# Two tiles' values together, output projections one or two steps later, and the head in a new order

## The chip, the cores and the metric

One core of one Trainium2 chip runs the program. It has five engines that work side by side, each with its own instruction queue: TensorE (PE, matmuls; its weight loads are PEld), VectorE (DVE), ScalarE (ACT), GpSimd (POOL) and SyncE (SP, which here only issues DMAs). The metric is the device time of one execution in microseconds.

## The reference

Two stages follow each other. The first is retention: causal attention whose scores are multiplied by a decay per head instead of a softmax. The second is a mixture of four attention experts, of which each token uses the two with the largest gate logits. The work here: 8 batches, 8 heads, 576 tokens, 64 numbers per head, 512 per token.

```
scores = scale * np.matmul(q, k.transpose(0, 1, 3, 2))
Dmat = np.where(rel >= 0, gamma[:, None, None] ** rel[None, :, :], 0.0)
x = np.matmul(scores * Dmat[None], v)          # to [8, 576, 512]

logits = x @ w_gate                            # top 2 of 4, softmax of the two: w, mask
for e in range(E):
    q, k, v = x @ wq[e], x @ wk[e], x @ wv[e]  # 64 wide
    scores = scale * (q @ k.transpose(0, 2, 1))
    a = softmax(causal(scores))
    ye = a @ v @ wo[e]
    out += mask[..., None] * w[:, :, kk:kk + 1] * ye
```

## The kernel before, in words

A batch of 576 tokens is cut into five chunks (128, 128, 128, 128 and 64 tokens), 40 chunks in all. For the projections it is cut into two ranges, the first of 256 tokens (chunks 0 and 1) and the second of 320 (chunks 2 to 4). The main loop (L506) runs over steps n = 0 to 41, and each step does something for several chunks:

- `load(n+2)` issues the DMAs of a later chunk on SP; `decay(n+1)` scales its `vk` by the decay (L106; GpSimd for n above 5, VectorE before), and in the first batch makes a piece of the table `gi` (L105).
- `qk(n)` multiplies queries and keys within blocks of 64 (L139), ScalarE evicts them to `p` (L142), GpSimd makes them causal (L145). `state(n)` (L119) sums up keys and values for later chunks (`st`, added into `s` at L127).
- `result(n-1)` finishes retention for the chunk before: `old` (L167, from `s`) and `own` (L177, from `p` and `vk`), added into x (L170, L182), times `gi` (L187), split into a high part `xh` (L188, ScalarE) and the rest `xl` (L189). It is a generator: the first part runs at the start of a step, the rest in its middle.
- `scores(m)` for the tile m = n - 6: the attention scores of 128 queries (`ss`, L318 or L327), VectorE's maximum (L339), ScalarE's exponential (L347); `normal(m)` scales the rows by the gate's weight over the sum (L369).
- `turn(m-1)`: the tile before is transposed on TensorE (`pt`, L382) and copied to `pth` (L385 on VectorE, L387 on ScalarE).
- `work(n)`: a table (L441) gives steps their projections. For batch b: k and q of the first range at step 5b+3 (`kq0`, L228), its values at 5b+5 (`v0`, L252), k and q of the second range at 5b+6, its values at 5b+7, output projection (`po`, L428, and DMA out) of the first range at 5b+9 and of the second at 5b+12. `vproj` also copies the gate's logits (`lg`, L257).
- `values(m-1)`: probabilities times values (`ys`, L403), evicted by ScalarE (L416) and split by GpSimd (L417, L418).

All four compute engines run their instructions in the order in which the code is written; a program adds only the semaphores for what depends on what. Every PSUM tile is one bank, and all take turns in the same eight banks (`bank`, L48):

```
    def bank(shape, name):
        return pool.tile(shape, F32, name=name, tag="b")
```

So the first matmul into a tile waits until the tile eight allocations earlier has been evicted. The names `x1h`, `x1l` are `xh` and `xl` of the second range. The engines' order in a step after the head is: `qk`, `old`, `own`, `st`, `ss`, `pt`, the step's projections, `ys`. The weights are cast by ScalarE (high part, L213) and subtracted by VectorE or GpSimd (low part, L214).

Of the kernel before, what the change touches and what calls it, by code (L numbers as in the profile page):

```python
# [8 lines left out]
F32 = mybir.dt.float32  # L9
# [19 lines left out]
def f(ap):  # L29
    return ap.bitcast(F32)  # L30
# [3 lines left out]
def kernel(ctx: ExitStack, tc: tile.TileContext, xf, xt, vkf, vkt,  # L34
# [61 lines left out]
    def decay(n):  # L96
        if n >= NC:
            return
        c = n % 5
        t0, C = CH[c]  # L100
        k = C // 64
        vv = VK[n][:, :, 0]
        if 0 < n < 5:
            for kc in range(4):
                act(gi[:, kc, t0:t0 + C], gi[:, kc, :C], AF.Copy, scale=fac[:, c, kc:kc + 1])  # L105
        (gp if n > 5 else v).tensor_mul(vv, vv, gam[:, 2 * c:2 * c + k].unsqueeze(3).to_broadcast([128, k, 4, D]))  # L106

    def state(n):
# [39 lines left out]
    def result(n):  # L148
        b, c = divmod(n, 5)
        t0, C = CH[c]  # L150
        q = 0 if c < 2 else 1
        q0, w, tiles = RNG[q]
        if c == tiles[0]:
            XR[b, q] = X1 if q else [sa.tile([128, 4, w], F32R, name="x" + y, bufs=1) for y in "hl"]
        xh, xl = XR[b, q]
        old = [bank([128, 2, C], "old") for g in range(2)]
        x, p, vk = X[n], P.pop(n), VK[n]
        x32 = sa.tile([128, 2, 2, C], F32, name="x32", tag="x32", bufs=2)
        f0 = 64 if c == 0 else 0
        for s in range(C // 64):  # L160
            k = 2 * c + s
            i = slice(64 * s, 64 * s + 64)
            if k:
                for r in range(2):
                    for g in range(2):
                        for u in range(2):
                            mm(old[g][HALF[u], r, i], S_[b, k - 1][HALF[g], r, u], x[HALF[g], 0, 2 * r + u, i],  # L167
                               start=True, stop=True)
        for g in range(2):
            act(x32[:, g, :, f0:], old[g][:, :, f0:], AF.Copy)  # L170
        own = [bank([128, 2, C], "own") for r in range(2)]
        for s in range(C // 64):
            i = slice(64 * s, 64 * s + 64)
            for g in range(2):
                for r in range(2):
                    for u in range(2):
                        mm(own[r][HALF[u], g, i], vk[HALF[r], s, 0, 2 * g + u], p[HALF[r], g, s, u],  # L177
                           start=True, stop=True)
        for r in range(2):
            if f0:  # L180
                v.tensor_copy(x32[:, :, r, :f0], own[r][:, :, :f0])
            v.tensor_add(x32[:, :, r, f0:], x32[:, :, r, f0:], own[r][:, :, f0:])  # L182
        x32 = x32.rearrange("p g r i -> p (g r) i")
        l0 = t0 - q0
        yield
        e = gp if n > 1 else v
        e.tensor_mul(x32, x32, gi[:, :, t0:t0 + C])  # L187
        act(xh[:, :, l0:l0 + C], x32, AF.Copy)  # L188
        e.tensor_sub(xl[:, :, l0:l0 + C], x32, f(xh[:, :, l0:l0 + C]))  # L189
        yield  # L190

# [10 lines left out]
        RAW[n] = raw = ld.tile([128, kc, w], F32, name="raw", bufs=3)  # L202
        nc.sync.dma_start(raw, wraw[:, o:o + kc * w].rearrange("p (k w) -> p k w", k=kc))

    def weights(n):
        o, kc, w = WCUT[n]
        raw = RAW[n]
        wt = w if n != "v" else NWV
        hi = const.tile([128, kc, wt], F32R, name="wh" + n)
        lo = const.tile([128, kc, wt], F32R, name="wl" + n)  # L210
        W[n] = (hi, lo)
        for r, cs in [(raw, slice(0, w))] + ([(rg, slice(w, wt))] if n == "v" else []):
            act(hi[:, :, cs], r, AF.Copy)  # L213
            (gp if n == "q" else v).tensor_sub(lo[:, :, cs], r, f(hi[:, :, cs]))  # L214

    def proj(b, r, w, p):
        r0, n, tiles = RNG[r]
# [20 lines left out]
    def vproj(b, r, t):  # L238
# [3 lines left out]
        l0, ti = t0 - r0, t - tiles[0]  # L242
        xh, xl = XR[b, r]
        if ti == 0:
            VN[b, r] = (sb.tile([128, nt, E * D], F32, name=f"vn{r}", bufs=2 - r),
                        sb.tile([128, nt, E], F32, name="lg", tag="lg"))
        vn, lg = VN[b, r]
        ps = bank([128, NWV], "pv")
# [122 lines left out]
    def turn(m):  # L371
        b, t = divmod(m, 5)
        p32, sm, n = SS.pop(m)
        nj = t + 1
        pth = sb.tile([128, n, nj, 128], F32, name="pth", tag="pth", bufs=2)
        PT[m] = pth
        for e in range(n):
            for j0 in range(0, nj, 4):
# [59 lines left out]
    for b in range(B):  # L438
        late = b == B - 1

        for n, kind in ((5 * b + 3, "kq0"), (5 * b + 5 - late, "v0"), (5 * b + 6, "kq1"), (5 * b + 7, "v1"),  # L441
                        (5 * b + 9 + (b == B - 2), "o0"), (5 * b + 12, "o1")):
            if b or kind[-1] == "1" or kind == "o0":
                STEPS.setdefault(n, []).append((b, kind, None))

# [51 lines left out]
            run(outproj(b, 1, d))  # L497

    warm(12)
    load(0)  # L500
    load(1)
    nc.sync.dma_start(gi[:, :, :128], gi_d)
# [3 lines left out]
    for n in range(NC + 2):  # L506
# [10 lines left out]
        if n < 3:  # L517

            next(late, None)
            qk(n)  # L520
            state(n)
            run(late)
        else:
            if n < NC:
                qk(n)
            next(late, None)
            if n < NC:
                state(n)
        soft = scores(new[0]) if new else iter(())
        turns = (None for m in old for _ in turn(m))  # L530
        for i, _ in enumerate(soft):
            if i:
                next(turns, None)
        run(late)
        decay(n + 1)
        run(turns)
        gates()
        for w in {1: "kq", 2: "v", 6: "o"}.get(n, ""):
            weights(w)
        for m in new[1:]:  # L540
            run(scores(m))
        for m in new:
            normal(m)
        run(work(n))
        for m in old:
            values(m)
    end()


# [53 lines left out]
```

## Time and profile before

| | us |
|---|---|
| median of 3 runs | 472.93 (472.51 to 473.53) |
| profiled execution | 470.27 |
| its span, first to last instruction | 468.5 |
| PE busy | 450.1 |
| DVE busy | 323.8 |
| ACT busy | 260.0 |
| POOL busy | 219.1 |

The profile is one execution. The span leaves out what lies around the first and the last instruction, so it is a little shorter than the execution's own time. Engine rows add up the time in which an engine had an instruction; a busy engine is not an engine at its best. One batch, five steps, takes some 54 us of the span.

### The profile page before, as it was taken

To read this page: it belongs to the slowest core of one execution; us is meant where nothing else is said; L and a number is where in the kernel's file an instruction comes from. 1 tells how busy PE (TensorE), PEld (TensorE's weight loads), DVE (VectorE), ACT (ScalarE), POOL (GpSimd) and SP (SyncE) were. 2 spreads that over 40 slices of the span, in tenths; PEclk is the share of its full clock that TensorE was granted. 3 is DMA by queue.
4 is the path that set the end of the run, shared out by engine and by line. 5 is a ranking of instruction groups with operands and counts; after the bars stand their busy time and mean duration, and the time that the engine had idled before them with its cause. 6 is when DMAs were issued, how large, how long until landed. Compare 5 with 4: busy or idle time off the path is not lost.

```text
span 468.5 us, 19045 instructions
## 1 busy us (share of the span) xinstructions
PE 450.1 (96%) x7996; PEld 398.9 (85%) x7996; DVE 323.8 (69%) x1136; ACT 260.0 (55%) x814; POOL 219.1 (47%) x285
## 2 busy tenths in 40 slices
PE   7497999999999999999999999999999999989996
PEld 4496988899879998899888998899988998777885
DVE  2644788766797668976687658976679657883662
ACT  2653666555666456645574555754565555663472
POOL 2437464644564454654455445654546544511100
PEclk9689999999999999999999999999999999999999
DMA  8946223314252243414233143512423110010031
GB/s 285 367 162 222 92 93 114 116 48 148 92 203 72 92 123 118 136 48 149 94 135 106 39 147 110 205 50 93 146 93 136 48 59 3 1 47 1 2 102 56
DMA packets 22516, 50.98 MB, mean 109 GB/s; under 512 B 2720, under 2 KB 11680, under 8 KB 22432
## 3 DMA queue, kind: packets, MB, share of 16 engines
q1 hardware_dynamic: 22432, 49.77, 30.7%
q8 instruction: 63, 1.03, 0.9%
q14 instruction: 21, 0.17, 0.1%
HBM read 40.33 MB, written 9.44 MB: 106 GB/s over the span
## 4 chain that ended last, share of the span: by engine, by line
PE 88%; DVE 3%; ACT 3%; POOL 2%; DMA 2%; issue 1%; SPq 0%; ACTq 0%; POOLq 0%; DVEq 0%
PE pj L228 22%; PE po L428 11%; PE pv L252 11%; PE pt L382 10%; PE ys L403 10%; PE ss L318 8%; PE qk L139 4%; PE ss L327 3%; PE own L177 3%; PE st L119 3%; PE old L167 3%; DMA gi<-gi 2%; POOL x L187 1%; DVE p L369 1%; ACT gi L105 1%
## 5 line engine op out<-in xcount | busy, mean ns | idle before, releaser
L347 ACT ACTIVATE p<-p,nm 128x128 f32<-128x128 f32 (+4 forms) x144 | 83.0, 578 | 79.2 <-DVE nm L339 57.7
L369 DVE TENSOR_SCALAR p<-p,sm 128x128 f32<-128x128 f32 (+4 forms) x144 | 78.9, 607 | 1.4
L417 POOL CAST yh<-y 128x256 fp32r<-128x256 f32 (+1 forms) x39 | 16.8, 430 | 109.6 <-ACT y L416 109.6
L339 DVE CUSTOM_DVE_ANT_0 p<-ss,mask 128x512 f32<-128x512 f32 (+3 forms) x128 | 56.4, 483 | 7.8 <-PE ss L318 7.3
L382 PEld LDWEIGHTS pt<-con,p 128*128 128x128 f32 x400 | 43.1, 141 | 20.5 <-issue 12.0
L145 POOL TENSOR_SCALAR_AFFINE_SELECT p<-p 64x512 f32<-64x512 f32 (+1 forms) x80 | 49.5, 619 | 22.7 <-ACT p L142 20.1
L182 DVE TENSOR_TENSOR x<-x,own 128x256 f32<-128x256 f32 (+1 forms) x80 | 26.4, 363 | 48.2 <-ACT x L170 46.7
L189 POOL TENSOR_TENSOR x1l<-x,x1h 128x512 fp32r<-128x512 f32 (+1 forms) x24 | 26.6, 1106 | 62.8 <-ACT x1h L188 62.8
L382 PE MATMUL pt<-con,p 128*128 128x128 f32 x400 | 52.8, 278 | 1.6 <-DVE nm L339 1.2
L403 PE MATMUL ys<-pth,vn 128*64 128x128 f32 (+1 forms) x960 | 53.0, 260 | 0.0
L403 PEld LDWEIGHTS ys<-pth,vn 128*64 128x64 f32 x960 | 44.3, 137 | 5.9 <-issue 1.5
L187 POOL TENSOR_TENSOR x<-x,gi 128x512 f32<-128x512 f32 (+1 forms) x38 | 44.7, 1177 | 4.1 <-DVE x L182 0.5
L318 PE MATMUL ss<-k,q 64*64 64x512 f32 (+3 forms) x512 | 42.5, 432 | 0.0
L385 DVE COPY pth<-pt 128x512 f32<-128x512 f32 (+3 forms) x80 | 37.9, 486 | 4.9 <-PE pt L382 4.4
L106 POOL TENSOR_TENSOR vk<-vk,con 128x512 f32<-128x512 f32 (+1 forms) x34 | 34.0, 1000 | 0.0
L387 ACT ACTIVATE pth<-pt 128x512 f32<-128x512 f32 (+3 forms) x80 | 33.1, 420 | 0.9 <-PE pt L382 0.8
L189 POOL TENSOR_TENSOR xl<-x,xh 128x512 fp32r<-128x512 f32 x14 | 18.8, 1342 | 31.5 <-ACT xh L188 31.5
L142 ACT ACTIVATE p<-qk 128x256 f32<-128x256 f32 (+1 forms) x80 | 24.6, 360 | 11.6 <-PE qk L139 11.6
L416 ACT ACTIVATE y<-ys 128x256 f32<-128x256 f32 (+1 forms) x39 | 14.2, 363 | 28.8 <-PE ys L403 28.8
L428 PE MATMUL po<-yh,who 128*128 128x320 f32 (+1 forms) x128 | 28.8, 306 | 0.6 <-ACT yh L412 0.6
L256 ACT ACTIVATE vn<-pv 128x256 f32<-128x256 f32 x40 | 15.1, 383 | 24.8 <-PE pv L252 24.8
L177 PE MATMUL own<-p,vk 64*64 64x64 f32 x1152 | 26.7, 223 | 2.0 <-issue 1.6
(112 smaller groups left out, 1044.7 us busy)
## 6 DMA issues: line engine op xcount, KB each, us to landing
x<-xf SPq DMA_DIRECT2D x32, 512.0 KB, 4.4
vk<-vkf SPq DMA_DIRECT2D x32, 512.0 KB, 5.4
out<-ot SPq DMA_DIRECT2D x32, 160.0 KB, 1.9
out<-ot SPq DMA_DIRECT2D x32, 128.0 KB, 1.8
raw<-wraw SPq DMA_DIRECT2D x4, 512.0 KB, 7.2
x<-xt SPq DMA_DIRECT2D x8, 256.0 KB, 2.8
vk<-vkt SPq DMA_DIRECT2D x8, 256.0 KB, 3.2
gi<-gi SPq DMA_DIRECT2D x1, 256.0 KB, 7.9
```

Of the source, the lines that this page charges most:

```text
L145: gp.affine_select(w, w, pattern=[[0, 4 * k], [1, 64]], base=0, channel_multiplier=-1, compare_op=OP.is_ge, fill=0.0)
L187: e.tensor_mul(x32, x32, gi[:, :, t0:t0 + C])
L189: e.tensor_sub(xl[:, :, l0:l0 + C], x32, f(xh[:, :, l0:l0 + C]))
L228: mm(ps, ww[:, kc, p * 128:(p + 1) * 128], xx[:, kc, :n], start=(i == 0), stop=(i == 11))
L252: mm(ps, xx[:, kc, l0:l0 + 128], ww[:, kc], start=(i == 0), stop=(i == 11))
L318: mm(ps[2 * p + z][HALF[i]], q[p][HALF[z], l0 + 64 * i:l0 + 64 * i + 64], k[p][HALF[z], :w], start=True, stop=True)
L339: v.tensor_tensor_reduce(p32[:, e], ps[e], mask[:, 512 - w:], -1.0, BIG, OP.add, OP.min, nm[:, e:e + 1])
L347: act(p32[:, e, :w], p32[:, e, :w], AF.Exp, bias=bias, scale=-1.0, accum_out=sm[:, 0, e:e + 1])
L369: v.tensor_scalar(p32[:, e, :t0 + C], p32[:, e, :t0 + C], rs[:, e:e + 1], None, op0=OP.mult)
L382: nc.tensor.transpose(pt[:, j - j0], p32[:, e, 128 * j:128 * j + 128], ident)
L403: mm(py[64 * z:64 * z + 64, p], VN[b, rr][0][:, j - 2 * rr, e * D:(e + 1) * D], src, start=(j == 0), stop=(j == t))
L428: mm(ps, ww[:, p, d * 128:(d + 1) * 128], yy[:, p], start=(i == 0), stop=(i == 5))
```

## The change

It has four parts.

1. `values` no longer runs for one tile at the end of every step. Tiles that have been transposed are collected in a list, and at the end of every odd step (and every step from 40) the values of all tiles in the list are computed one after another. `pth` gets a third buffer, `vn1` a second.
2. The output projections move: the first range's from step 5b+9 to 5b+10, the second range's from 5b+12 to 5b+14.
3. In the first five steps the scaling of `gi` moves from `decay` into `result`, behind the eviction of `old`; the rest of `result` has one more break and, up to step 5, runs at the end of a step.
4. The weights of k and q are split into the casts (`"h"`) and the subtractions (`"l"`), and are made in step 2 instead of 1, those of v in step 3 instead of 2.

```diff
@@ -100,9 +100,6 @@
         t0, C = CH[c]
         k = C // 64
         vv = VK[n][:, :, 0]
-        if 0 < n < 5:
-            for kc in range(4):
-                act(gi[:, kc, t0:t0 + C], gi[:, kc, :C], AF.Copy, scale=fac[:, c, kc:kc + 1])
         (gp if n > 5 else v).tensor_mul(vv, vv, gam[:, 2 * c:2 * c + k].unsqueeze(3).to_broadcast([128, k, 4, D]))
 
     def state(n):
@@ -168,6 +165,9 @@
                                start=True, stop=True)
         for g in range(2):
             act(x32[:, g, :, f0:], old[g][:, :, f0:], AF.Copy)
+        if 0 < n < 5:
+            for kc in range(4):
+                act(gi[:, kc, t0:t0 + C], gi[:, kc, :C], AF.Copy, scale=fac[:, c, kc:kc + 1])
         own = [bank([128, 2, C], "own") for r in range(2)]
         for s in range(C // 64):
             i = slice(64 * s, 64 * s + 64)
@@ -186,6 +186,7 @@
         e = gp if n > 1 else v
         e.tensor_mul(x32, x32, gi[:, :, t0:t0 + C])
         act(xh[:, :, l0:l0 + C], x32, AF.Copy)
+        yield
         e.tensor_sub(xl[:, :, l0:l0 + C], x32, f(xh[:, :, l0:l0 + C]))
         yield
 
@@ -202,16 +203,18 @@
         RAW[n] = raw = ld.tile([128, kc, w], F32, name="raw", bufs=3)
         nc.sync.dma_start(raw, wraw[:, o:o + kc * w].rearrange("p (k w) -> p k w", k=kc))
 
-    def weights(n):
+    def weights(n, parts="hl"):
         o, kc, w = WCUT[n]
         raw = RAW[n]
         wt = w if n != "v" else NWV
-        hi = const.tile([128, kc, wt], F32R, name="wh" + n)
-        lo = const.tile([128, kc, wt], F32R, name="wl" + n)
-        W[n] = (hi, lo)
+        if "h" in parts:
+            W[n] = [const.tile([128, kc, wt], F32R, name="w" + y + n) for y in "hl"]
+        hi, lo = W[n]
         for r, cs in [(raw, slice(0, w))] + ([(rg, slice(w, wt))] if n == "v" else []):
-            act(hi[:, :, cs], r, AF.Copy)
-            (gp if n == "q" else v).tensor_sub(lo[:, :, cs], r, f(hi[:, :, cs]))
+            if "h" in parts:
+                act(hi[:, :, cs], r, AF.Copy)
+            if "l" in parts:
+                (gp if n == "q" else v).tensor_sub(lo[:, :, cs], r, f(hi[:, :, cs]))
 
     def proj(b, r, w, p):
         r0, n, tiles = RNG[r]
@@ -242,7 +245,7 @@
         l0, ti = t0 - r0, t - tiles[0]
         xh, xl = XR[b, r]
         if ti == 0:
-            VN[b, r] = (sb.tile([128, nt, E * D], F32, name=f"vn{r}", bufs=2 - r),
+            VN[b, r] = (sb.tile([128, nt, E * D], F32, name=f"vn{r}"),
                         sb.tile([128, nt, E], F32, name="lg", tag="lg"))
         vn, lg = VN[b, r]
         ps = bank([128, NWV], "pv")
@@ -372,7 +375,7 @@
         b, t = divmod(m, 5)
         p32, sm, n = SS.pop(m)
         nj = t + 1
-        pth = sb.tile([128, n, nj, 128], F32, name="pth", tag="pth", bufs=2)
+        pth = sb.tile([128, n, nj, 128], F32, name="pth", tag="pth", bufs=3)
         PT[m] = pth
         for e in range(n):
             for j0 in range(0, nj, 4):
@@ -439,7 +442,7 @@
         late = b == B - 1
 
         for n, kind in ((5 * b + 3, "kq0"), (5 * b + 5 - late, "v0"), (5 * b + 6, "kq1"), (5 * b + 7, "v1"),
-                        (5 * b + 9 + (b == B - 2), "o0"), (5 * b + 12, "o1")):
+                        (5 * b + 10, "o0"), (5 * b + 14, "o1")):
             if b or kind[-1] == "1" or kind == "o0":
                 STEPS.setdefault(n, []).append((b, kind, None))
 
@@ -497,6 +500,7 @@
             run(outproj(b, 1, d))
 
     warm(12)
+    TURNED = []
     load(0)
     load(1)
     nc.sync.dma_start(gi[:, :, :128], gi_d)
@@ -517,7 +521,10 @@
         if n < 3:
 
             next(late, None)
+            if n == 2:
+                weights("k", "h")
             qk(n)
+            next(late, None)
             state(n)
             run(late)
         else:
@@ -531,19 +538,24 @@
         for i, _ in enumerate(soft):
             if i:
                 next(turns, None)
-        run(late)
+        if n > 5:
+            run(late)
         decay(n + 1)
         run(turns)
         gates()
-        for w in {1: "kq", 2: "v", 6: "o"}.get(n, ""):
-            weights(w)
+        for w in {2: "kq", 3: "v", 6: "o"}.get(n, ""):
+            weights(w, "l" if w == "k" else "hl")
         for m in new[1:]:
             run(scores(m))
         for m in new:
             normal(m)
         run(work(n))
-        for m in old:
-            values(m)
+        run(late)
+        TURNED.extend(old)
+        if n % 2 or n >= NC:
+
+            while TURNED:
+                values(TURNED.pop(0))
     end()
```

What the new order does on ScalarE in the head, steps 0 to 2. Before (`gi` is the decay table, `wh..` a weight's high part, `x<-old` the eviction of `old`):

```order
L105 ACTIVATE gi<-gi,con 128x128 x4
L170 ACTIVATE x_183<-old 128x2x64 x2
L142 ACTIVATE p<-qk 128x256 x2
L188 ACTIVATE xh<-x_183 128x4x128
L105 ACTIVATE gi<-gi,con 128x128 x4
L213 ACTIVATE whk<-raw 128x1024
L213 ACTIVATE whq<-raw 128x1024
L170 ACTIVATE x_285<-old 128x256 x2
L142 ACTIVATE p<-qk 128x256 x2
L188 ACTIVATE xh<-x_285 128x4x128
```

After:

```order
L167 ACTIVATE x_179<-old 128x2x64 x2
L139 ACTIVATE p<-qk 128x256 x2
L188 ACTIVATE xh<-x_179 128x4x128
L167 ACTIVATE x_269<-old 128x256 x2
L170 ACTIVATE gi<-gi,con 128x128 x4
L215 ACTIVATE whk<-raw 128x1024
L139 ACTIVATE p<-qk 128x256 x2
L188 ACTIVATE xh<-x_269 128x4x128
L215 ACTIVATE whq<-raw 128x1024
L236 ACTIVATE k_371<-pj 128x256
```

The eviction `x_285<-old` stood behind a scaling of `gi` and both weight casts; now (as `x_269<-old`) it is ahead of them, and the second cast comes behind the next `xh`.

TensorE at the end of step 12 and the start of step 13, before (the last value projections, then one tile's values, then the next step):

```order
L252 MATMUL pv<-whv,x1l 128x260 x4
L252 MATMUL pv<-whv,x1h 128x260 x4
L252 MATMUL pv<-wlv,x1h 128x260 x4
L252 MATMUL pv<-whv,x1l 128x260 x4
L403 MATMUL ys<-pth,vn_1660 64x128 x4
L139 MATMUL qk<-x 64x64 x16
L167 MATMUL old<-x,s 64x64 x16
L177 MATMUL own<-p,vk 64x64 x16
L119 MATMUL st<-vk 64x64 x16
```

After:

```order
L255 MATMUL pv<-whv,x1l 128x260 x4
L255 MATMUL pv<-whv,x1h 128x260 x4
L255 MATMUL pv<-wlv,x1h 128x260 x4
L255 MATMUL pv<-whv,x1l 128x260 x4
L136 MATMUL qk<-x 64x64 x16
L164 MATMUL old<-x,s 64x64 x16
L177 MATMUL own<-p,vk 64x64 x16
L116 MATMUL st<-vk 64x64 x16
```

The `ys` row has gone from between the value projections and `qk`; the twelve rows of output projection (`po`) that stood ahead of the value projections in this step are gone as well.

TensorE at the end of step 14 and the start of step 15, before (end of the first range's output projection, values, next step):

```order
L428 MATMUL po<-yl_2184,who 128x256 x2
L428 MATMUL po<-yh_2183,wlo 128x256 x2
L403 MATMUL ys<-pth,vn_1660 64x128 x4
L403 MATMUL ys<-pth,vn_2130 64x128 x2
L403 MATMUL ys<-pth,vn_1660 64x128 x4
L403 MATMUL ys<-pth,vn_2130 64x128 x2
L139 MATMUL qk<-x 64x64 x16
L167 MATMUL old<-x,s 64x64 x8
L177 MATMUL own<-p,vk 64x64 x8
L119 MATMUL st<-vk 64x64 x16
```

After:

```order
L431 MATMUL po<-yh_1481,wlo 128x320 x2
L431 MATMUL po<-yh_1481,who 128x320 x2
L431 MATMUL po<-yl_1482,who 128x320 x2
L431 MATMUL po<-yh_1481,wlo 128x320 x2
L136 MATMUL qk<-x 64x64 x16
L164 MATMUL old<-x,s 64x64 x8
L177 MATMUL own<-p,vk 64x64 x8
L116 MATMUL st<-vk 64x64 x16
```

The projection is now that of the second range (320 columns for 256), and `qk` follows it with no `ys` between.

## Rows read from the trace of the kernel before

**Rows 1.** The page: engine table (busy us, share of the span, instructions) and the shares of the chain of waits by engine.

```profile
PE 450.1 (96%) x7996; PEld 398.9 (85%) x7996; DVE 323.8 (69%) x1136; ACT 260.0 (55%) x814; POOL 219.1 (47%) x285
...
PE 88%; DVE 3%; ACT 3%; POOL 2%; DMA 2%; issue 1%; SPq 0%; ACTq 0%; POOLq 0%; DVEq 0%
```

**Rows 2.** Busy time by stretch. Columns: the stretch in us, its length; busy us and instructions (in brackets) of PE, PEld, DVE, ACT and POOL in this order, the granted clock, the DMA share and GB/s. The first two rows are stretches of the head; the last is the sum over five stretches that together are one batch (254.84 to 309.10 us).

```profile
16.33:26.57 10.24, 6.08 (x104) 5.77 (x96) 7.72 (x14) 7.03 (x17) 4.10 (x3) 0.50 0.87 310
26.58:45.00 18.42, 15.23 (x491) 14.05 (x489) 6.69 (x24) 7.96 (x28) 12.29 (x15) 1.00 0.59 202
...
sum 54.26, PE 54.26 PEld 48.87 DVE 39.91 ACT 31.25 POOL 28.33; mean PE 10.85 PEld 9.77 DVE 7.98 ACT 6.25 POOL 5.67
```

**Rows 3.** Timeline of TensorE: groups of value matmuls (`ys`) and the instructions that follow them. Columns here and in all groups below: start us, length us, engine, line, operation, written<-read, shape, count, and in brackets the idle time before and what ended it.

```profile
223.94 0.66 PE L403 MATMUL ys<-pth,vn 128*64 128x128 f32 x8
224.52 0.69 PE L139 MATMUL qk<-x 64*64 64x64 f32 x32
...
234.66 1.09 PE L403 MATMUL ys<-pth,vn 128*64 128x128 f32 x16
235.69 0.46 PE L139 MATMUL qk<-x 64*64 64x64 f32 x16
...
243.07 1.53 PE L403 MATMUL ys<-pth,vn 128*64 128x128 f32 x24
244.53 0.69 PE L139 MATMUL qk<-x 64*64 64x64 f32 x32
...
429.73 1.82 PE L403 MATMUL ys<-pth,vn 128*64 128x64 f32 x48
431.49 1.95 PE L318 MATMUL ss<-k,q 64*64 64x512 f32 x16
```

**Rows 4.** Timeline of TensorE and GpSimd in step 9 and at the start of step 10 (`po` is the first range's output projection of batch 0).

```profile
73.83 1.93 PE L318 MATMUL ss<-k,q 64*64 64x512 f32 x15
76.98 0.48 PE L428 MATMUL po<-yh,who 128*128 128x256 f32 x2
80.00 1.53 PE L403 MATMUL ys<-pth,vn 128*64 128x128 f32 x24
81.25 1.23 POOL L106 TENSOR_TENSOR vk<-vk,con 128x512 f32<-128x512 f32 x1
82.53 0.69 PE L119 MATMUL st<-vk 64*64 64x64 f32 x32
```

**Rows 5.** Step 24 and the start of step 25, TensorE and GpSimd; below them two rows of step 22 (a second-range output projection, the value projection after it).

```profile
236.91 1.93 PE L318 MATMUL ss<-k,q 64*64 64x512 f32 x15
244.33 1.22 POOL L106 TENSOR_TENSOR vk<-vk,con 128x512 f32<-128x512 f32 x1
245.61 0.69 PE L119 MATMUL st<-vk 64*64 64x64 f32 x32
...
215.93 0.53 PE L428 MATMUL po<-yh,who 128*128 128x320 f32 x2
219.53 0.64 PE L252 MATMUL pv<-whv,x1h 128*128 128x260 f32 x4
```

**Rows 6.** Step 22 and the start of step 23 (TensorE and VectorE), and below them the `own` matmuls of step 8.

```profile
214.33 1.08 PE L318 MATMUL ss<-k,q 64*64 64x256 f32 x15
222.13 0.15 DVE L257 COPY lg<-pv 128x4 f32<-128x4 f32 x1
225.51 0.65 PE L177 MATMUL own<-p,vk 64*64 64x64 f32 x31
...
62.38 0.75 PE L177 MATMUL own<-p,vk 64*64 64x64 f32 x30 [0.38 <-DVE lg L257]
```

**Rows 7.** The scaling of p by row (VectorE L369): for a tile of 128 keys in step 6, for one of 256 in step 7, and GpSimd's subtraction beside the latter.

```profile
52.42 0.87 DVE L369 TENSOR_SCALAR p<-p,sm 128x128 f32<-128x128 f32 x4
...
59.06 3.10 DVE L369 TENSOR_SCALAR p<-p,sm 128x256 f32<-128x256 f32 x4
59.17 1.39 POOL L189 TENSOR_TENSOR xl<-x,xh 128x512 fp32r<-128x512 f32 x1 [2.71 <-ACT xh L188]
```

**Rows 8.** Head: steps 1 and 2 on VectorE, ScalarE and TensorE.

```profile
16.80 0.69 DVE L106 TENSOR_TENSOR vk<-vk,con 128x512 f32<-128x512 f32 x1
15.89 1.26 ACT L105 ACTIVATE gi<-gi,con 128x128 f32<-128x128 f32 x4
18.95 0.63 ACT L170 ACTIVATE x<-old 128x256 f32<-128x256 f32 x2
19.61 0.75 DVE L182 TENSOR_TENSOR x<-x,own 128x256 f32<-128x256 f32 x2 [0.26 <-ACT x L170]
21.08 1.04 DVE L187 TENSOR_TENSOR x<-x,gi 128x512 f32<-128x512 f32 x1
22.21 0.63 ACT L188 ACTIVATE xh<-x 128x512 fp32r<-128x512 f32 x1 [2.08 <-DVE x L187]
22.89 1.23 PE L228 MATMUL pj<-xh,whk 128*128 128x256 f32 x4 [4.16 <-ACT xh L188]
24.96 1.05 PE L228 MATMUL pj<-xh,wlk 128*128 128x256 f32 x4
27.67 0.69 PE L139 MATMUL qk<-x 64*64 64x64 f32 x32
```

**Rows 9.** TensorE in steps 4 and 5: two waits.

```profile
38.66 0.68 PE L119 MATMUL st<-vk 64*64 64x64 f32 x28 [1.56 <-DVE lg L257]
...
43.94 0.69 PE L119 MATMUL st<-vk 64*64 64x64 f32 x32 [1.63 <-POOL vk L106]
```

## The prediction

> **What bounds the kernel now.** I read the engine table and the chain of waits first [rows 1]. TensorE is busy 450.1 of 468.5 us, and the chain that ends last is TensorE for 88%: no other engine is a bound on average. Next the busy times by stretch [rows 2]. One batch (five steps) takes 54.26 us, in which TensorE works all the time and VectorE, the next, 39.91 us. Only the head is loose: from 16.33 to 26.57 us TensorE works 6.08 of 10.24 us at a granted clock of 0.50 (its level of 1.2 GHz), and from 26.58 to 45.00 it works 15.23 of 18.42 us. So the change can win TensorE instructions in the steady part and waits in the head. It can lose wherever a step becomes so short on TensorE that another engine is no longer hidden. I therefore looked, step by step, at how late the other engines' results arrive, and expect two such places.
>
> **Values together (A).** A group of value matmuls is followed at once by the next group, so starts can be subtracted [rows 3]: 8 matmuls take 224.52 - 223.94 = 0.58 us, 16 take 235.69 - 234.66 = 1.03, 24 take 244.53 - 243.07 = 1.46. That is 0.44 per 8 and a fixed 0.14 to 0.15 per group. In the tail a group of 48 narrow ones takes 431.49 - 429.73 = 1.76, so length adds no second fixed part. Over steps 7 to 39 there are 33 groups now and 17 after. One of the 16 lost groups belongs to term B, and 15 x 0.15 = 2.2 us saved. The buffers cost nothing: transposed p lives one step longer and has a third buffer, the second range's values have a second one.
>
> **The first batch's output projection (B).** It moves from step 9 to 10, and nothing else is issued in step 9. Now [rows 4] scores start at 73.83, the projection at 76.98 and the values at 80.00, so it takes 3.02 us; `st` of step 10 starts at 82.53. GpSimd's decay of the `vk` that it reads ends at 81.25 + 1.23 = 82.48, which is 8.65 after the scores began. That end doesn't depend on the projection: decay stands on GpSimd behind `xl`, which waits for the ScalarE cast `xh`, which is queued behind the exponentials of this step's scores. So the stretch from scores to `st` stays 8.70 us long though 3.0 us of work leave it, and that work is added to step 10. One tile's values (16 matmuls, 1.03) leave step 8 and fall into the hole in step 9. Net +1.9 us.
>
> **Steps 14, 24, 34 (C).** They lose the first-range projection and one tile's values and get the second-range projection. In step 24 [rows 5] scores start at 236.91, decay ends at 244.33 + 1.22 = 245.55 (again 8.64 later) and `st` starts at 245.61, so even now there is no slack. After the change TensorE needs from scores to `st`: 3.15 up to the projection (76.98 - 73.83), 219.53 - 215.93 = 3.60 for a second-range projection, and 245.61 - 244.53 = 1.08 for `qk`, `old` and `own`; 7.83 in all. It waits 8.70 - 7.83 = 0.87 each time: 3 x 0.87 = +2.6 us. Bounds: nothing, if decay comes earlier by that much; 3 x 1.5, if the chain in front of it slips by one more ScalarE operation of 0.63 (as long as the cast `xh` in [rows 8]).
>
> **Steps 12, 22, 32 (D).** Here the second-range projection leaves and the values go to the odd step, so only three value projections remain. The output of step 22 [rows 6] is the case. Scores start at 214.33; 1.60 later comes what is now the projection and then will be the value projections, which take 223.94 - 219.53 = 4.41; `own` follows 225.51 - 224.52 = 0.99 after `qk`. `own` could start at 221.33. But all PSUM tiles take turns in eight banks, and without a `ys` tile in between `own` falls on the bank of the first value projection. That bank is free when VectorE has copied the gate logits (`lg`), at 222.13 + 0.15 = 222.28, behind the scaling of the whole tile by row. Behind `own` on TensorE stand `st` and the scores. A precedent is in the trace: `own` at 62.38, after a step that has no output projection, waits 0.38 for just that copy. So I price it between 0.38 and 1.0 and take 0.9, nearer to the worked case: 3 x 0.9 = +2.7 us.
>
> **A rule against the last step of that argument.** While GpSimd's subtraction runs (59.17 for 1.39 us), four scalings of 128x256 take 3.10 us; four of 128x128 with no GpSimd beside them take 0.87 [rows 7]. Twice the length costs 3.6 times as much. The Trainium skill, "SBUF — State Buffer", Who interferes with whom, says that a VectorE operation in a two-port mode and a GpSimd operation lock one shared port pair, and the later one blocks fully until the other is done; the rows agree with it. By that rule `lg` would be about 3.10 - 2 x 0.87 = 1.4 us earlier once the subtraction no longer meets the scaling, and D would vanish. I don't expect the meeting to be undone, as both hang on the same exponentials; it is rival two.
>
> **The head (G).** Now [rows 8] ScalarE brings gi(1) (from 15.89), two weight casts and only then `x<-old` at 18.95, so `x<-x,own` starts on VectorE at 19.61, the product with gi at 21.08, `xh` at 22.21 and the projection at 22.89. After the change `x<-old` is ahead of these; VectorE's first free moment is the end of `vk` at 17.49. With the same durations: 17.49 + 0.7 + 1.04 + 0.63 = 19.9, so the projection starts 2.9 earlier. It doesn't keep all of it: its third group needs `wlk`, which VectorE now makes after `s`, `xl` and `vk`, at about 22.9 instead of before 24.96. The last 16 matmuls took 27.67 - 24.96 = 2.71 and 24.96 - 22.89 = 2.07 per 8 at the lower clock, so they end at 25.6 to 27.0; I take 26.2, a gain of 1.5. Up to step 6, waits of 1.56 (`lg`) and 1.63 (`vk`) on TensorE [rows 9] lie open, but the ScalarE to GpSimd chain of `x`, `xh` and the causal select is nearly as long, and I give that stretch 0.5. G = -2.0 us (-1.3 to -3.3).
>
> **Sum.** -2.2 + 1.9 + 2.6 + 2.7 - 2.0 = +3.0 us. The profiled execution took 470.27 us (span 468.5), so its copy would take 473.3. The median of the runs is 472.93, 2.66 more, and the forecast is for a median: 475.9 us. Of the rest I cost at nothing: the odd steps get longer on TensorE, so nothing else can be late there; SP issues the same loads two steps ahead, behind outputs that now come later; the tail is the same code.
>
> **Rivals.**
> 1. Faster: the waits B to D don't open, because the chains of decay and `lg` start earlier than the scores seem to say. Then -2.2 - 2.0 = -4.2 leaves about 468.7, with B's projection moved at no cost. For it: GpSimd is busy 28.33 and VectorE 39.91 of 54.26 us [rows 2], so each has idle time to move into. Against it: `st` starts 0.05 to 0.06 behind decay's end in [rows 4, 5] alike, so it is held already. Chance 0.14.
> 2. No change: D vanishes (the scaling no longer meets the subtraction), 475.9 - 2.7 = 473.2. For it: the size of the slow-down in [rows 7]. Against it: both engines wait for the same ScalarE cast order. Chance 0.13.
> 3. Slower by more: the head gives only 0.7 and the holes grow to 1.5 each in C and D, because ScalarE now gets the evictions of two values tiles at once and the exponentials behind them slip. -2.2 - 0.7 + 1.9 + 4.5 + 4.5 = +8.0, 480.9. It decides from the point at which the first exponential of an even step waits for a `y` eviction and not for VectorE's maximum. Chance 0.05.
> 4. The change doesn't pair at all. The written order fixes 17 groups, so no chance.
>
> **The numbers.** The forecast has 0.68, with its own range 473.5 to 478.5. I widen below to 472.0 for rival two and leave out the rest: 472.0 to 478.8. A measurement tells about 0.2% (0.95 us) from no change, so faster gets 0.14 (rival one), the same 0.14 (rival two and the weakest of the forecast), slower 0.72.
>
> **What would show it.** Right: 17 groups of `ys`; `own` of steps 13, 23 and 33 idle about 0.9 us behind `lg`; `st` of steps 10, 15, 25 and 35 idle behind `vk`; the first projection near 20 us and `qk` after it at 25.6 to 27. Wrong: no idle time ahead of these, a pair of batches not some 1 us longer than 108.5, or a head that gives back 4 us.

## The result and the profile after

The changed kernel took 476.07 us (median of 6 runs, 475.23 to 478.38), the kernel before 473.05 in the same comparison (471.71 to 473.53): ratio 1.0084, 95% interval 1.0064 to 1.0105. It is slower by 3.0 to 5.0 us. Profiled execution against profiled execution it is 475.23 against 470.27, +4.96.

The page after, to be held against [rows 1]:

```profile
PE 447.6 (95%) x7996; PEld 399.0 (84%) x7996; DVE 327.6 (69%) x1136; ACT 260.4 (55%) x814; POOL 220.2 (46%) x285
...
PE 73%; DVE 10%; ACT 9%; POOL 3%; DMA 2%; issue 2%; SPq 0%; DVEq 0%; POOLq 0%; ACTq 0%
```

TensorE is busy 2.5 us less, as values in pairs should make it, yet its share of the chain that ends last fell from 88% to 73%; VectorE and ScalarE have most of the rest. TensorE now waits for the other engines. From the start of step 7 to that of step 39 (columns as in [rows 2]), before:

```profile
52.23:398.43 346.20, 345.82 (x6398) 311.51 (x6397) 255.90 (x904) 199.59 (x634) 180.55 (x228) 1.00 0.31 105
```

and after:

```profile
52.04:399.48 347.44, 340.51 (x6357) 307.86 (x6357) 257.26 (x904) 197.69 (x629) 181.79 (x228) 1.00 0.31 103
```

TensorE idled 0.38 us there and now idles 6.93. Where it waits, its timeline says (columns as in [rows 3]; steps 9 and 10, then the starts of 13, 15, 23 and 33):

```profile
78.31 0.88 PE L406 MATMUL ys<-pth,vn 128*64 128x128 f32 x12 [0.54 <-ACT pth L390]
81.39 0.69 PE L116 MATMUL st<-vk 64*64 64x64 f32 x32 [1.11 <-POOL vk L103]
...
115.24 0.62 PE L177 MATMUL own<-p,vk 64*64 64x64 f32 x26 [0.47 <-DVE lg L260]
...
135.78 0.69 PE L116 MATMUL st<-vk 64*64 64x64 f32 x32 [0.69 <-POOL vk L103]
...
225.19 0.62 PE L177 MATMUL own<-p,vk 64*64 64x64 f32 x26 [1.21 <-DVE lg L260]
...
335.09 0.62 PE L177 MATMUL own<-p,vk 64*64 64x64 f32 x26 [1.21 <-DVE lg L260]
```

With 0.65 and 0.68 for `st` of steps 25 and 35, not shown, these waits add up to 6.56 us. The waits for `vk` and for `lg` are the two kinds that the forecast named, at its places; the 0.54 for a copy of transposed p in step 9 it did not name. The rows that answer to [rows 6, 7], VectorE and GpSimd in step 22:

```profile
221.54 3.44 DVE L372 TENSOR_SCALAR p<-p,sm 128x256 f32<-128x256 f32 x4
224.90 0.28 DVE L260 COPY lg<-pv 128x4 f32<-128x4 f32 x3
...
221.65 1.39 POOL L190 TENSOR_TENSOR xl<-x,xh 128x512 fp32r<-128x512 f32 x1 [2.71 <-ACT xh L188]
222.99 1.09 POOL L103 TENSOR_TENSOR vk<-vk,con 128x512 f32<-128x512 f32 x1
224.17 1.37 POOL L142 TENSOR_SCALAR_AFFINE_SELECT p<-p 64x512 f32<-64x512 f32 x2
```

The same step in the kernel before:

```profile
219.25 2.96 DVE L369 TENSOR_SCALAR p<-p,sm 128x256 f32<-128x256 f32 x4
...
219.36 1.39 POOL L189 TENSOR_TENSOR xl<-x,xh 128x512 fp32r<-128x512 f32 x1 [2.71 <-ACT xh L188]
220.71 1.09 POOL L106 TENSOR_TENSOR vk<-vk,con 128x512 f32<-128x512 f32 x1
```

In both the scaling lies beside two GpSimd operations, the subtraction and the decay. Now it also runs into a third, the causal select of the next step, and is 0.48 us longer. The head, answering to [rows 8]:

```profile
20.97 3.37 DVE L217 TENSOR_TENSOR wlk<-raw,whk 128x1024 fp32r<-128x1024 f32 x1
...
20.44 2.81 POOL L217 TENSOR_TENSOR wlq<-raw,whq 128x1024 fp32r<-128x1024 f32 x1 [0.53 <-POOL p L142]
...
19.40 1.22 PE L231 MATMUL pj<-xh,whk 128*128 128x256 f32 x4 [1.11 <-ACT xh L188]
...
24.39 1.22 PE L231 MATMUL pj<-xh,wlk 128*128 128x256 f32 x4 [2.67 <-DVE wlk L217]
...
28.02 0.69 PE L136 MATMUL qk<-x 64*64 64x64 f32 x32
```

The first projection does start 3.5 us earlier, and then waits 2.67 us for `wlk`, so that `qk` of step 3 comes at 28.02 instead of 27.67. Step 7 begins at 52.04 (52.23 before): of the head's gain 0.2 us is left in this pair of traces. All of the loss is behind it: from step 7 to the end 421.46 us instead of 416.27.

### The profile page after: what moved, and what is told of

Its sections match the earlier page's. It is cut to its first block, busy times and chain, and to the rows that moved or that the text cites. A ratio compares the mean times of both kernels' runs of the same rounds, so it can differ in the third digit from the quotient of the medians.

```text
span 473.5 us, 19049 instructions
## 1 busy us (share of the span) xinstructions
PE 447.6 (95%) x7996; PEld 399.0 (84%) x7996; DVE 327.6 (69%) x1136; ACT 260.4 (55%) x814; POOL 220.2 (46%) x285
## 4 chain that ended last, share of the span: by engine, by line
PE 73%; DVE 10%; ACT 9%; POOL 3%; DMA 2%; issue 2%; SPq 0%; DVEq 0%; POOLq 0%; ACTq 0%
PE pj L231 21%; PE ys L406 9%; PE po L431 9%; PE pt L385 8%; PE pv L255 8%; PE ss L321 5%; ACT p L350 5%; PE ss L330 3%; DVE p L372 3%; PE qk L136 3%; PE own L177 3%; PE st L116 2%; DMA vk<-vkf 2%; DVE x L182 2%; PE old L164 2%
## 5 line engine op out<-in xcount | busy, mean ns | idle before, releaser
L372 DVE TENSOR_SCALAR p<-p,sm 128x128 f32<-128x128 f32 (+4 forms) x144 | 84.3, 645 | 1.4
L142 POOL TENSOR_SCALAR_AFFINE_SELECT p<-p 64x512 f32<-64x512 f32 (+1 forms) x80 | 50.5, 632 | 54.1 <-ACT p L139 51.0
L420 POOL CAST yh<-y 128x256 fp32r<-128x256 f32 (+1 forms) x39 | 15.8, 404 | 76.2 <-ACT y L419 76.1
L406 PE MATMUL ys<-pth,vn 128*64 128x128 f32 (+1 forms) x960 | 49.7, 258 | 0.6 <-ACT pth L390 0.5
L103 POOL TENSOR_TENSOR vk<-vk,con 128x512 f32<-128x512 f32 (+1 forms) x34 | 35.0, 1029 | 0.1
L390 ACT ACTIVATE pth<-pt 128x512 f32<-128x512 f32 (+3 forms) x80 | 33.1, 420 | 0.9 <-PE pt L385 0.8
L116 PE MATMUL st<-vk 64*64 64x64 f32 x1024 | 22.9, 224 | 6.4 <-POOL vk L103 3.6
```

The lines of the kernel that those rows point to most:

```text
L142: gp.affine_select(w, w, pattern=[[0, 4 * k], [1, 64]], base=0, channel_multiplier=-1, compare_op=OP.is_ge, fill=0.0)
L372: v.tensor_scalar(p32[:, e, :t0 + C], p32[:, e, :t0 + C], rs[:, e:e + 1], None, op0=OP.mult)
L406: mm(py[64 * z:64 * z + 64, p], VN[b, rr][0][:, j - 2 * rr, e * D:(e + 1) * D], src, start=(j == 0), stop=(j == t))
```

## The experiments

Each was timed beside the kernel before; ratios are to that. The kernel before had medians of 471.7, 472.9 and 471.7 us in the three sets, so ratios are compared, not times; the changed kernel's, 1.0084, comes from the comparison above.

**wlq on VectorE.**

```diff
-                (gp if n == "q" else v).tensor_sub(lo[:, :, cs], r, f(hi[:, :, cs]))
+                v.tensor_sub(lo[:, :, cs], r, f(hi[:, :, cs]))
```

> The changed kernel, with the low part of q's weights (wlq) subtracted on VectorE behind wlk, not on GpSimd beside it. Theory: in the head of the changed kernel wlk takes 3.37 us (1.22 before) only because GpSimd's wlq runs from 20.44 to 23.25 and holds VectorE up. Then wlk takes 1.2 to 1.3 here, the third group of projections starts near 22.2 instead of 24.39, the qk behind it at 25.6 to 26.3 instead of 28.02, and the kernel is 1.7 to 2.3 us faster than the changed one (473.8 to 474.4). Rival: wlk is slow by itself (its size, or the ScalarE cast whq beside it): it still takes over 3 us, wlq comes after it, the last group starts later still, and the kernel is 0 to 1 us slower than the changed one.

Measured: 474.36 us, ratio 1.0060 (1.0037 to 1.0082), 0.24% or 1.1 us better than the changed kernel. VectorE and TensorE in its head:

```profile
21.16 1.21 DVE L217 TENSOR_TENSOR wlk<-raw,whk 128x1024 fp32r<-128x1024 f32 x1
...
22.42 1.23 PE L231 MATMUL pj<-xh,wlk 128*128 128x256 f32 x4 [0.40 <-DVE wlk L217]
...
26.14 0.96 PE L136 MATMUL qk<-x 64*64 64x64 f32 x32
```

`wlk` takes 1.21 us, and the projection and `qk` come within 0.25 us of what was expected. Step 7 begins at 50.47, 1.6 earlier. The medians show less than that and less than the 1.7 to 2.3 expected, and their intervals overlap. More traces bear the gain out: from the start of step 2 to that of step 7 the four with `wlq` on VectorE, this one and three below, take 33.1 to 34.6 us, the five with the new head and `wlq` on GpSimd 35.0 to 36.2. So the cause is shown, the size, some 1.4, only roughly.

**Decay early.**

```diff
         if n > 5:
+            next(late, None)
+            decay(n + 1)
             run(late)
-        decay(n + 1)
+        else:
+            decay(n + 1)
```

> The changed kernel, with GpSimd's decay of vk (steps from 6) between the product with gi and the subtraction xl, where GpSimd waits 3 us for ScalarE's cast. Theory: st of steps 10, 15, 25 and 35 waits only for this decay; its idle times of 1.11, 0.69, 0.65 and 0.68 go and the kernel is 2.5 to 3.5 us faster than the changed one (472.6 to 473.6); in step 9 up to 0.6 stays, because the values still wait for a copy of transposed p. Rival: the decay now runs beside VectorE's maxima or scalings and slows them, so that lg and own come later: gain under 1 us, with own of steps 13, 23, 33 idle more than now (0.47, 1.21, 1.21).

Measured: 469.85 us, ratio 0.9948 (0.9932 to 0.9964): 1.36% or 6.4 us better than the changed kernel, twice what was expected. Steps 7 to 39 take 340.22 us instead of 347.44. Not only the waits for `vk` went. GpSimd, VectorE and TensorE in step 22:

```profile
216.85 1.05 POOL L103 TENSOR_TENSOR vk<-vk,con 128x512 f32<-128x512 f32 x1
219.61 1.38 POOL L190 TENSOR_TENSOR xl<-x,xh 128x512 fp32r<-128x512 f32 x1 [1.72 <-ACT xh L188]
...
219.50 2.17 DVE L372 TENSOR_SCALAR p<-p,sm 128x256 f32<-128x256 f32 x4
221.59 0.28 DVE L260 COPY lg<-pv 128x4 f32<-128x4 f32 x3
...
221.66 0.85 PE L177 MATMUL own<-p,vk 64*64 64x64 f32 x30
```

With the decay out of its way the same scaling takes 2.17 us and ends before the next select begins, `lg` is in time and `own` waits for nothing. Summed over the kernel, the page's group of the scaling, first of the changed kernel:

```profile
L372 DVE TENSOR_SCALAR p<-p,sm 128x128 f32<-128x128 f32 (+4 forms) x144 | 84.3, 645 | 1.4
```

and with the early decay:

```profile
L372 DVE TENSOR_SCALAR p<-p,sm 128x128 f32<-128x128 f32 (+4 forms) x144 | 66.0, 518 | 1.4
```

The rival (the decay slows the maxima instead) falls.

**Value projections ahead of the scaling.**

```diff
+        job = work(n)
+        if n > 5 and n % 5 == 2 and n % 2 == 0:
+            run(job)
         for m in new:
             normal(m)
-        run(work(n))
+        run(job)
```

> The changed kernel, where in steps 12, 22 and 32 the value projections with their copies of the gate logits (lg) are written ahead of the scaling of p by row, on VectorE thus ahead of it. TensorE's own order is the same. Theory: own of steps 13, 23, 33 waits for lg alone, which stands behind the scaling; its idle times (0.47, 1.21, 1.21) go, and the kernel is 2.5 to 3.6 us faster than the changed one (472.5 to 473.6). Rival: the scaling, now about 1.5 us later, becomes what the transposes of the next step wait for, and the wait moves from own to pt: gain under 1 us.

Measured: 477.36 us, ratio 1.0111 (1.0086 to 1.0136): no gain, if anything a loss. The rival holds. VectorE and TensorE in step 23:

```profile
225.14 1.60 DVE L372 TENSOR_SCALAR p<-p,sm 128x256 f32<-128x256 f32 x4
226.67 0.74 DVE L182 TENSOR_TENSOR x<-x,own 128x256 f32<-128x256 f32 x2
...
227.13 0.77 PE L385 MATMUL pt<-con,p 128*128 128x128 f32 x4 [0.70 <-DVE x L182]
```

`own` is free (223.97), but VectorE still scales when `own` and the scores are done, and the transposes wait. The wait has moved one phase on.

**All three.** The three edits above in one kernel.

> The three edits of the runs beside it in one kernel. If each takes away its own wait and they do not meet, the gains add up: 6.7 to 9.4 us less than the changed kernel, 467 to 469, below the kernel before (473). Rival: with less idle time in TensorE other results come late in turn, and the sum is at most 4 us, about level with the kernel before.

Measured: 470.86 us, ratio 0.9975 (0.9956 to 0.9993), worse than the early decay alone. Between the starts of steps 12 and 14 it takes 21.7 us where the early decay alone takes 20.2: the early decay has already taken away the wait of `own` that the edit before this one was to win back, so only its cost is left. Beside the next run, which lacks that edit, it is 1.0% slower. The gains did not add up: it is 5.2 us faster than the changed kernel, between the theory's 6.7 to 9.4 and the rival's 4.

**wlq and early decay, without the third edit.**

> The changed kernel with two edits: wlq on VectorE behind wlk, and GpSimd's decay of vk ahead of the subtraction xl. Theory: the head gains what it gained alone (1.1 by the medians, about 1.9 by the trace) and the decay what it gained alone (about 6), so the kernel stands 3 to 4.5 us under the kernel before (ratio 0.990 to 0.994). Rival: in the head the gain is eaten up by the later steps 3 to 6, as they wait for GpSimd anyway, and it is no faster than the run with the decay alone (ratio 0.9948).

Measured: 466.59 us, ratio 0.9873 (0.9851 to 0.9895), 6.0 us below the kernel before and the best of all, below the 0.990 to 0.994 expected. The gain is larger than the two alone (0.24% and 1.36% on 1.0084 make 0.9923), by no more than the intervals of the runs add up to. Its chain is TensorE's again:

```profile
PE 88%; DMA 3%; DVE 3%; ACT 3%; POOL 1%; SPq 1%; issue 0%; POOLq 0%; DVEq 0%; ACTq 0%
```

**The early decay in three steps only** (12, 22, 32, where `st` doesn't wait for it).

```diff
-        if n > 5:
-            run(late)
-        decay(n + 1)
+        if n > 5 and n % 10 == 2:
+            next(late, None)
+            decay(n + 1)
+            run(late)
+        else:
+            if n > 5:
+                run(late)
+            decay(n + 1)
```

> The changed kernel with the early decay in steps 12, 22 and 32 alone; there st does not wait for it. Theory of the port: the scaling of p by row is slow (3.44 us for four of 128x256) because it meets two GpSimd operations, the subtraction and the decay; with one of them gone it takes 2.1 to 2.3, lg is about 1.3 earlier, the idle times of own in steps 13, 23, 33 (0.47, 1.21, 1.21) fall to 0.2 or less, and the kernel is 2.5 to 3.5 us faster than the changed one. Waits of st at steps 10, 15, 25, 35 stay as they are. Rival: the scaling is slow by its size; it takes 3 us or more, own waits as before, and the gain is under 0.7.

Measured: 473.26 us, ratio 1.0020 (1.0003 to 1.0036), 0.64% or 3.0 us better than the changed kernel. VectorE and TensorE, first the untouched wait of step 10, then step 22:

```profile
81.11 0.69 PE L116 MATMUL st<-vk 64*64 64x64 f32 x32 [1.11 <-POOL vk L103]
...
223.22 0.85 PE L177 MATMUL own<-p,vk 64*64 64x64 f32 x30
...
221.06 2.17 DVE L372 TENSOR_SCALAR p<-p,sm 128x256 f32<-128x256 f32 x4
```

This is the cleanest of the tests: in these steps no instruction waits for the decay's own result, and taking it out of the scaling's way alone ends the idle time of `own` in all three (0.47, 1.21 and 1.21 in the changed kernel).

**The early decay in the kernel before.** The same edit there, with the break between `xh` and `xl`.

> The kernel before, with only GpSimd's decay of vk (steps from 6) ahead of the subtraction xl. Theory: the early decay is worth something only where a step is too short on TensorE; the kernel before has one recorded wait of that kind after the head (own at 62.38 behind lg, 0.38 us), so it gains 0.3 to 1.0 us (ratio 0.998 to 0.9995). Rival: the decay is a hidden bound of the kernel before too, as its st follows decay by 0.05 us in every short step; then it gains 2 to 4 us (ratio 0.992 to 0.996) and the change is slower even beside the best of its fixes.

Measured: 470.39 us, ratio 0.9954 (0.9938 to 0.9970), in the rival's range. The trace shows less: steps 7 to 39 take 345.66 us (346.20 before), and step 8 alone is 0.67 shorter, although the scaling falls from 78.9 to 65.6 us in this kernel too. Where the rest of the 2.2 us lies, one trace of each doesn't tell; it stays open. So part of what the early decay gives has nothing to do with the change: beside a kernel before that has it too (0.9954), the changed kernel with it (0.9948) is level, and only the run with `wlq` moved as well (0.9873) is ahead.

**The fixed kernel without pairs** (values at the end of every step).

> The fixed kernel (wlq on VectorE, early decay) with the values of one tile at the end of every step, as in the kernel before; head and moved projections stay. Theory: pairing is worth the start of 16 groups, 16 x 0.15, so this is 2.0 to 2.6 us slower than the fixed kernel with pairs. Rival: pairs cost as much elsewhere (the values of two tiles wait for the copy of transposed p in step 9, 0.54 us, and the even steps are short), and it is 0 to 1 us slower.

Measured: 470.09 us, ratio 0.9944 (0.9922 to 0.9965), 0.71% or 3.3 us slower than with pairs. The 2.4 expected for the pairs and 0.8 in step 9 make up the difference: there the values of tile 2 now wait twice for the copies of transposed p, 1.35 us in sum instead of 0.55:

```profile
74.20 0.88 PE L406 MATMUL ys<-pth,vn 128*64 128x128 f32 x12 [0.44 <-ACT pth L390]
75.98 0.88 PE L406 MATMUL ys<-pth,vn 128*64 128x128 f32 x12 [0.91 <-ACT pth L390]
```

**The moves alone**, in the kernel before.

```diff
-                        (5 * b + 9 + (b == B - 2), "o0"), (5 * b + 12, "o1")):
+                        (5 * b + 10, "o0"), (5 * b + 14, "o1")):
```

> The kernel before, with only the output projections moved (first range to step 5b+10, second to 5b+14); values after each step and the old head. Theory: the moves open the holes, the pairs save starts and deepen some holes. Step 9 without a projection: scores to st still 8.70 us, the hole 3.0. Steps 12, 17, 22, 27, 32, 37 have value projections and one tile's values only, like step 7 before: own waits 0.4 to 0.6 behind lg each, 2.4 to 3.6. Steps 14 to 39 with a projection of 320 columns and values are long enough: nothing. So 5.4 to 6.6 us slower than the kernel before (ratio 1.011 to 1.014). Rival: the pairs are what opens the holes; the moves alone cost at most the 3.0 of step 9 (ratio under 1.0065).

Measured: 477.68 us, ratio 1.0124 (1.0104 to 1.0144), as the theory had it. `own` waits for `lg` in the six steps behind those that it named, 0.19 to 0.39 us each. TensorE in steps 9, 10 and 23:

```profile
77.24 0.88 PE L403 MATMUL ys<-pth,vn 128*64 128x128 f32 x12 [0.43 <-ACT pth L387]
79.02 0.88 PE L403 MATMUL ys<-pth,vn 128*64 128x128 f32 x12 [0.91 <-ACT pth L387]
82.09 0.69 PE L119 MATMUL st<-vk 64*64 64x64 f32 x32 [1.09 <-POOL vk L106]
...
226.33 0.81 PE L177 MATMUL own<-p,vk 64*64 64x64 f32 x32 [0.39 <-DVE lg L257]
```

**The pairs with the least moves**, in the kernel before, with the buffers of part 1.

```diff
+                        (5 * b + (9 if b % 2 else 10), "o0"), (5 * b + (13 if b % 2 else 12), "o1")):
...
+        TURNED.extend(old)
+        if n % 2 or n >= NC:
+            while TURNED:
+                values(TURNED.pop(0))
```

> The kernel before, with only the pairs, and output projections moved no further than the pairs need: first range 5b+10 for even b (5b+9 else), second range 5b+13 for odd b (5b+12 else). Theory: 16 starts saved, -2.4; step 9 as in the changed kernel, +1.9; steps 14, 24, 34 have a projection of 256 columns and no values, 3.15 + 3.02 + 1.08 = 7.25 of 8.70 us, so st waits 1.45 each, +4.4; steps 12, 22, 32 keep a projection, nothing. Together +3.9 (ratio 1.007 to 1.010), with st of steps 15, 25, 35 idle by 1.2 to 1.5 behind vk. Rival: without the far moves the pairs gain: -0.5 to -2.4 (ratio under 0.999).

Measured: 480.28 us, ratio 1.0177 (1.0155 to 1.0199), the slowest of all and 4.4 us beyond the theory's +3.9. The waits of 1.3 to 1.4 are there (step 15), but I had overlooked that steps 19 and 29 lose their projection as step 9 does. That makes two more holes of some 1.9 us, like the first one. TensorE in steps 15, 19 and 20:

```profile
140.00 0.69 PE L119 MATMUL st<-vk 64*64 64x64 f32 x32 [1.36 <-POOL vk L106]
...
191.26 0.88 PE L403 MATMUL ys<-pth,vn 128*64 128x128 f32 x12 [0.54 <-ACT pth L387]
194.34 0.69 PE L119 MATMUL st<-vk 64*64 64x64 f32 x32 [1.11 <-POOL vk L106]
```

The far moves of the change are thus the milder form: they keep some work in these steps.

**The head alone**, in the kernel before (parts 3 and 4 of the change).

> The kernel before, with only the new head (order of gi and of the weights); values after each step, projections at their old steps. Theory: the earlier start of the first projection is given back because wlk waits for GpSimd's wlq; qk of step 3 comes at 27 to 28.5 us as in the changed kernel, and the time is -0.5 to +0.5 against the kernel before (ratio 0.999 to 1.001), with wlk at 3.2 to 3.5 us. Rival (my forecast): the head alone gains 1.3 to 3.3 us (ratio 0.993 to 0.997), and the loss came later.

Measured: 471.06 us, ratio 0.9993 (0.9978 to 1.0007). My forecast for the head falls (the interval leaves room for 1.0 us of gain, not for 1.3); the giving back is shown by the same pair of rows, VectorE and GpSimd:

```profile
21.14 3.37 DVE L217 TENSOR_TENSOR wlk<-raw,whk 128x1024 fp32r<-128x1024 f32 x1
...
20.61 2.81 POOL L217 TENSOR_TENSOR wlq<-raw,whq 128x1024 fp32r<-128x1024 f32 x1 [0.54 <-POOL p L142]
```

**The kernel before once more.**

> The kernel before once more, for a second profile, since its profiled execution (470.27) is one of its shortest and its runs reach from 470.2 to 474.0. Theory: the spread is made in the head, by how long TensorE stays at the lower clock: from step 7 on both traces agree within 0.3 us, and a longer execution has its whole difference ahead of 52 us. Rival: in longer executions waits open in the steps as well (own behind lg, st behind vk); then the stretch from step 7 to step 39 (346.2 us in the first trace) is longer by most of the difference.

Measured: ratio 1.0005 (0.9988 to 1.0023), profiled execution 472.27, 2.0 longer than the first one. Steps 7 to 39 agree within 0.1 us (346.30), the head is 0.4 longer, and 1.6 lie where neither theory had them, behind step 39. Two stretches there, columns as in [rows 2], first of the first trace:

```profile
420.00:425.00 5.00, 3.45 (x23) 2.92 (x22) 4.03 (x19) 3.49 (x13) 0.43 (x1) 1.00 0.13 44
425.00:430.00 5.00, 5.00 (x41) 4.81 (x41) 0.28 (x2) 1.04 (x4) 0.00 (x0) 1.00 0.01 3
```

and of the second:

```profile
420.00:425.00 5.00, 3.45 (x20) 2.92 (x19) 3.87 (x19) 3.04 (x12) 0.81 (x2) 0.87 0.20 68
425.00:430.00 5.00, 5.00 (x29) 5.00 (x28) 0.75 (x3) 0.88 (x2) 0.00 (x0) 0.79 0.01 3
```

## Why the prediction was right, and where it was not

The range and the sign held, and 475.9 stands beside 476.07. Of the signs named, a pair of batches (steps 22 to 32) takes 109.90 us instead of 108.53. The steps were not all that good.

**A, values together: right.** The trace has the 17 expected groups. The run without pairs is 3.3 us slower, as 2.4 for 16 starts and 0.8 in step 9 would make it; the starts were not timed apart from the rest.

**B, the empty step 9: right.** Steps 8 to 10 take 30.92 us (30.93 before) although one tile's values, 1.90, have left for step 11: +1.9. The hole is divided between the values, which wait 0.54 for a copy of transposed p, and `st`.

**C, `st` behind the decay: right.** In step 14 `st` starts 8.71 after the scores (127.07 to 135.78; 8.70 forecast). From the start of `own` to `st` it takes 1.1 us where it took 0.33 before (245.28 to 245.61), some 0.8 more in each of three steps, 2.4 in all (forecast 2.6).

**D, `own` behind `lg`: right in kind, too small.** `own` takes 0.7, 1.4 and 1.4 us more (2.7 forecast, 3.5 measured). The step that failed is the one that took the end of `lg` over from the trace before, 7.95 us after the scores. It came 8.4 after them (216.62 to 225.05), because the scaling took 3.44 instead of 2.96. In the trace before it already lay beside the subtraction and the decay. What is new is the causal select: the step is now so short that the select of the next one starts at 224.17, while the scaling runs. In step 12, where the scaling takes 2.97 as before, `own` waits only 0.47.

The prediction also read the 3.10 us of [rows 7] as the cost of the subtraction alone; in that trace the decay (60.52 to 61.61) lay beside it too. So rival two had the mechanism (the scaling meeting GpSimd sets D), but more of GpSimd takes part in it, and the change doesn't undo the meeting. The early decay undoes most of it. Beside the subtraction alone the scaling takes 2.17, beside subtraction and decay 2.96, with the select behind them 3.44, and 1.60 in the run with the projections first, where only the end of the select lies beside it.

Rival three's larger holes came in part, in D, but not by its way: the first exponential of step 22 waits for VectorE's maximum (2.01 us), not for a `y` eviction.

**G, the head: wrong.** -2.0 was forecast, -0.2 came in this pair of traces. Five traces with the old head take 35.6 to 36.2 us from step 2 to step 7 and five with the new one 35.0 to 36.2, so the gain is some 0.4 in the mean and within the spread. The start of the first projection (19.9 forecast, 19.40 measured) and the 0.5 of steps 3 to 6 (24.56 us before, 24.02 after) were right. What failed is the sentence that `wlk` is made "at about 22.9": it is priced there by its length of 1.2 in the trace before. It ends at 24.34, because GpSimd's `wlq`, which before started 1.06 behind it, now starts 0.53 ahead of it. The run with `wlq` on VectorE shows it; the head alone shows the same rows again.

I weighed the Trainium skill, "SBUF — State Buffer", Who interferes with whom, for the scaling alone. The same section says that a VectorE operation with two inputs in SBUF contends with a GpSimd operation that reads SBUF. That is `wlk` beside `wlq`, and the trace agrees: `wlk` ends 1.09 us after `wlq` (24.34 and 23.25), and again 1.09 after it in the head alone (24.51 and 23.42). By this rule the head's gain was to be had only if the two were kept apart, as in the run with `wlq` on VectorE.

**The sum.** With A as forecast and the other terms as measured, -2.2 + 1.9 + 2.4 + 3.5 - 0.2 is +5.4; the scores of step 40 take 2.06 instead of 2.58, which leaves +4.9 beside the +4.96 of the traces. My sum was +3.0. That the median came out right is luck: the 2.66 that I added from the profiled execution to the median belonged in part to that one execution of the kernel before: the profiled execution of the changed kernel is only 0.84 below its median. Two errors of some 1.9 us cancelled.

## What to carry to other kernels

Before work is moved out of a step, find what that step hides: if another engine's result already arrives with 0.05 us to spare, each microsecond moved out is added in full where it lands. Moving an instruction also moves what it runs beside; an operation's length in the trace before holds only for its neighbours there, so price VectorE operations again where GpSimd works at the same time. And where one engine is idle waiting, look for a later operation of its own queue that can go there: one early decay turned a loss of 0.8% into a gain of 0.5%, and with `wlq` moved into one of 1.3%. Try such a fix on the old kernel as well: there the same early decay gained 0.5% too.

## What was not expected of the hardware

TensorE's granted clock fell in the tail of one profiled execution of the kernel before and not of the other. In both TensorE had waited 1.20 us for VectorE just before; in one it went on at 1.00, in the other at 0.87 and 0.79 as means of two stretches of 5 us (the levels being 2.4 and 1.2 GHz). The projections that followed, 48 matmuls, took 8.74 instead of 7.21 us. This is 1.5 of the 2.0 us between these two executions. The same 1.20 us wait stands in the trace of the head alone, with 0.86 and 0.80 in the same two stretches, and in that of the changed kernel, with 1.00 throughout. A single profiled execution can thus lie 1.5 us off for this alone. That it is part of the 2.66 above is likely but not shown, as only two executions of the kernel before left a trace.
